# Attention with exponentials on two engines: a score ring of five PSUM banks and scores on demand for VectorE

## The chip, the cores and the metric

The kernel runs on one core of a Trainium2 chip. The time is that of one execution on the device, in microseconds (us). It is given as the median over several runs; beside it stands one execution that the hardware profiler recorded, with its own time. Most executions of one kernel agree within 0.3%.

## What is computed

The input is cut to what matters. S = 2048 rows, width D = 448, 16 heads of 28 columns, feed-forward width 1792, everything in bfloat16.

```python
xn = layernorm(x)
q, k, v = split(xn @ wqkv)                     # 16 heads of 28
p = softmax(q @ k.T * 28 ** -0.5)              # 2048 x 2048 a head
s = (p @ v).merge_heads() @ wo
g = silu(gelu(xn @ w1 + b1) @ w2 + b2)
out = x + s * g
```

## The kernel before

**Tiles.** A *score tile* is 128 keys by 512 queries of one head, as large as one PSUM bank. There are 16 blocks, one for each of 4 groups of 4 heads and 4 chunks of 512 queries; a block has 16 key tiles for each of its 4 heads, 64 score tiles. So there are 1024 of them, numbered m in the order of work, with block m // 64 and head m % 4. In the last block the tiles are cut by queries, so that its last quarters end one after another. For each tile TensorE computes the scores (line 1156), an engine takes the exponential, and TensorE multiplies it with the values and adds it into one accumulating bank, `acc` (PV, line 1389). At the end of a block VectorE copies `acc` out (line 1441) and the *epilogue* divides by the sums.

**Two engines take exponentials.** ScalarE does it in one ACTIVATE over several banks at once (line 1195), from the score ring to places in the buffer `P` (21 of them). VectorE does it for some tiles, called *late*, in four steps: it reads the bank and scales it into a buffer `y` (line 1218, 1309 for eight tiles), and then makes three passes over a pair of tiles (lines 1331, 1332, 1334), which leave the exponentials in one of five pair buffers `plate`. There are two `y` buffers, and one pair is in its three passes at a time.

**The ring.** PSUM has eight banks. Six are the ring, used as two sets of three: while ScalarE reads one set, TensorE fills the other. One is `acc`, and one, `misc`, is the *side bank*, for which all other work queues up: projections (line 722), values (976), feed-forward (1034, 1092), epilogues and the output projection (1480). The units of the ring are a fixed list, `UNITS`: two tiles each for the first 64 tiles (while banks 2 and 3 still serve the start), three behind them. When a unit is filled, `pick_late` may give its last tile to VectorE: then ScalarE's call covers two tiles, VectorE reads the third bank, and the set is free when both are done. At least three units lie between the two tiles of a pair. Eight late tiles are fixed beforehand (`MPAIRS`) and use the side bank, in block 9, where ScalarE does the gelus.

**The order of the work** is made when the kernel is built. Each part is a generator (`p_scores`, `p_exps`, `p_late`, `p_pv`, ...) that yields tasks with an engine, buffers, an estimated duration and a rank; a planner keeps a clock per engine, and puts next the task that can start first, by rank among those within 0.1 us of it. Each engine then runs its own list in that order, with semaphores between them. Late tiles are chosen by estimates: `backlog()` is VectorE's work that is due, `THS` has a limit on it for each block, and `SLACKS` says for each block how far VectorE may end behind ScalarE. Where TensorE would be idle for long by the planner, `p_busy` puts in keep-warm matmuls that add zero to `acc` (line 884).

**The gelu stretch.** In block 9, from tile GM = 582 on, ScalarE does all gelus together (line 1071): eight pieces from SBUF, and seven of three banks straight from the six banks of the ring (`p_direct`). Later `p_silu` uses tanh, which is in one table set with exp.

Of the kernel before, what the change touches and what calls it, by code (L numbers as in the profile page):

```python
# [24 lines left out]
UB = 3  # L25
# [6 lines left out]
MPAIRS = [tuple(64 * 9 + x for x in p) for p in ((16, 21), (26, 31), (36, 41), (46, 51))]  # L32
MLATE = set(m for ms in MPAIRS for m in ms)
_seq = [m for m in range(64, MTOT) if m not in MLATE]
UNITS = [list(range(m, m + 2)) for m in range(0, 64, 2)] + [_seq[i:i + UB] for i in range(0, len(_seq), UB)]
GU = min(u for u, ms in enumerate(UNITS) if ms[-1] >= GM)
RB, RPREV, UOF, UBASE, _last = {}, {}, {}, [], {}
for _u, _ms in enumerate(UNITS):
    UBASE.append(4 * (_u % 2) if _u < 32 else 3 * (_u % 2))
    for _k, _m in enumerate(_ms):  # L40
        UOF[_m] = _u
        RB[_m] = UBASE[_u] + _k
        RPREV[_m] = _last.get(RB[_m])
        _last[RB[_m]] = _m
for _m in sorted(MLATE):
    UOF[_m] = UOF[_m - 1]
LATE_GAP, LATE_SUB = 3, 15
LC = 1.85
THS = (5.0, 7.0, 15.0, 8.0, 8.0, 8.0, 8.0, 6.0, 8.0, 8.0, 8.0, 8.0, 8.0, 8.0, 8.0, 8.0)
SLACKS = (2.0, 2.0, 6.0, 2.0, -1.0, 2.0, 2.0, 2.0, 2.0, 1.0, 2.0, 2.0, 2.0, 4.5, 2.0, 2.0)  # L50
NU = len(UNITS)
# [24 lines left out]


class _Pair:
    __slots__ = ("i", "u", "ms", "done", "closed")

    def __init__(self, i, u, m):
        self.i, self.u, self.ms, self.done, self.closed = i, u, [m], 0, False
# [14 lines left out]
class _Kernel:  # L97
# [101 lines left out]

    def settle(self):  # L200
        again = True
        while again:
            again = False
            for p in sorted(self.procs, key=lambda p: (p[0], p[1])):
                op = p[3]
                if isinstance(op, _Task):
                    continue
                if op[0] == "until" and op[1]():
                    self.advance(p)
                    again = True  # L210
                elif op[0] == "bank" and self.banks and (len(op) < 2 or op[1]()):
                    i = min(range(len(self.banks)), key=lambda i: max(self.banks[i][1].tr, self.banks[i][1].tw or 0))
                    self.advance(p, self.banks.pop(i))
                    again = True
# [52 lines left out]
    def alloc(self):  # L267
# [60 lines left out]
        self.b_P = [B() for _ in range(NP)]  # L328
# [14 lines left out]
        self.b_xnT = [[B(), B()] for _ in range(C)]  # L343
        self.b_wqkf = B()
# [24 lines left out]
        self.b_dum = B()  # L369
        self.b_nm = [[B(), B()] for _ in range(C)]  # L370
# [13 lines left out]
    def schedule(self):  # L384
# [6 lines left out]
        K.sc_late = -1  # L391
        K.pv_u = -1
# [11 lines left out]
        K.ring6 = False  # L404
        K.taken = 0
        K.ring_rel = [False] * MTOT
        K.pv_done = [False] * MTOT
        K.late = set(MLATE)
        K.late_left = [len([m for m in MLATE if K.sub_of(m) == b]) for b in range(NBLK + 3)]
        K.late_q = deque()  # L410
        K.late_on = False
        K.open = None
        K.dve_q = 0.0
        K.PB, K.PPREV, K.plast, K.pptr = {}, {}, {}, 0
        K.act_ms, K.p0 = [None] * NU, [0] * NU
# [15 lines left out]
        K.spawn(K.p_take(3), 0)  # L431
# [4 lines left out]
        K.spawn(K.p_mlate(), 0)  # L436
# [433 lines left out]
    def pe_low(self):  # L870
        K = self
        now = max(K.tE[PE], K.now)
        while K.pe_hist and K.pe_hist[0][1] < now - HAM_WIN:
            K.pe_hist.popleft()
        return sum(b - max(a, now - HAM_WIN) for a, b in K.pe_hist) < (HAM_LOW if K.exp_u < NU - 20 else 1.1) * HAM_WIN

    def p_busy(self):
        K = self
        yield ("until", lambda: K.pv_u >= 0)
# [8 lines left out]
        while K.exp_u < NU - 2:  # L888
            yield ("until", lambda: K.pe_low() or K.exp_u >= NU - 2)
# [149 lines left out]
    def p_direct(self):  # L1039
        K = self  # L1040
        s0 = UBASE[GU - 1]
        for i, (c, f0) in enumerate(DIRECT):
            b0 = (s0 + 3 * i) % NRING
            yield ("until", lambda: K.exp_u >= GU - 1 + i if i < 2 else K.dir_read >= i - 1)
# [5 lines left out]
    def p_gelu(self):  # L1050
        K = self
        yield ("until", lambda: K.exp_u >= GU and K.n_f1 == len(SBT))
        left = [FT] * C
        s0 = UBASE[GU - 1]
        for q, pc in enumerate(PIECES):
# [4 lines left out]
            else:  # L1060
                i = K.dir_read
                yield ("until", lambda: K.dir_n > i)
# [78 lines left out]

    def p_scores(self):
        K = self
        for u in range(NU):
            ms = UNITS[u]
            fl, fm, rd = [], [], []
            ps = [(m,) + K.pieces(m) for m in ms]
            for k in range(4):
                for m, b, j, pc, _, _ in ps:
                    if k >= len(pc):  # L1150
                        continue
                    t, q0, nq, col = pc[k]
                    g, c = b // C, b % C

                    def f(eng, m=m, t=t, j=j, g=g, c=c, q0=q0, nq=nq, col=col):
                        return eng.matmul(K.ring[:, RB[m], col:col + nq],  # L1156
                                          K.kT[32 * j:32 * j + 32, g, t * 128:(t + 1) * 128],
                                          K.qT[32 * j:32 * j + 32, g, c * 512 + q0:c * 512 + q0 + nq],
                                          tile_position=(32 * j, 0), start=True, stop=True)
                    fl.append(f)  # L1160
                    fm.append(m)
                    rd += [K.b_qT[g][c], K.b_kT0 if (g, t // 2) == (0, 0) else K.b_kT[g][t // 4]]

            if len(ms) == 3 and not K.ring6:
                yield ("until", lambda: K.taken == 2)
                K.ring6 = True
            if u == GU + 1:
                yield ("until", lambda: K.dir_read == len(DIRECT))
            yield ("until", lambda: all(RPREV[m] is None or K.ring_rel[RPREV[m]] for m in ms))
            K.assign(u)  # L1170
            dur = 0.17 + 0.05 * len(ms) + 0.005 * (len(fl) - len(ms))
            for part in ([ms[-1:], ms[:-1]] if len(K.act_ms[u]) < len(ms) else [ms]):
                fp = [f for f, m in zip(fl, fm) if m in part]

                def fall(eng, fp=fp):
                    ins = None
                    for f in fp:
                        ins = f(eng)
                    return ins
                d = dur if part is ms else 0.12 if len(part) == 1 else dur - 0.12  # L1180
                yield _Task(PE, fall, rd, [K.b_ring[RB[m]] for m in part], d, 0.1, 1)
                if len(part) == 1:
                    K.sc_late = u
            K.sc_u = u

    def p_exps(self):
        K = self
        for u in range(NU):
            yield ("until", lambda: K.sc_u >= u)
            ms, b0, p0 = K.act_ms[u], UBASE[u], K.p0[u]  # L1190
            n = len(ms)
            yield ("until", lambda: all(K.PPREV[m] is None or K.pv_done[K.PPREV[m]] for m in ms))

            def fexp(eng, b0=b0, p0=p0, n=n):
                return eng.activation(K.P[:, p0:p0 + n, :], K.ring[:, b0:b0 + n, :], ACTF.Exp, scale=SM_SCALE)  # L1195
            yield _Task(ACT, fexp, [K.b_ring[b0 + k] for k in range(n)], [K.b_P[p0 + k] for k in range(n)],
                        0.0725 + 0.4267 * n, 0.08, 3)
            for m in ms:
                K.ring_rel[m] = True
            K.exp_u = u  # L1200
            K.exp_m = UNITS[u + 1][0] - 1 if u + 1 < NU else MTOT - 1
            if u >= NU - 2:
                for k in range(n):
                    K.banks.append((K.ring[:, b0 + k, :], K.b_ring[b0 + k]))

    def p_late(self):
# [6 lines left out]
        while K.sc_u < NU - 1 or K.late_q:  # L1213
            yield ("until", lambda: K.sc_u == NU - 1 or (K.late_q and UOF[K.late_q[0][0]] <= max(K.sc_u, K.sc_late)))
            if not K.late_q:
                return
            m, i, half, pair = K.late_q.popleft()
            yield _Task(DVE, lambda eng, m=m, i=i, half=half: eng.tensor_scalar(  # L1218
                K.ysb[i][:, 512 * half:512 * half + 512], K.ring[:, RB[m], :], SM_SCALE * LOG2E * 128.0,
                127.0 * 128.0, op0=ALU.mult, op1=ALU.add),  # L1220
                        [K.b_ring[RB[m]]], [K.b_y[i][half]], 0.69, 0.0, 1)
            K.dve_q -= 0.69
            K.ring_rel[m] = True
            pair.done += 1
            if pair.closed and pair.done == len(pair.ms):
                K.spawn(K.p_exp2(tuple(pair.ms), i), m)
# [11 lines left out]
    def close(self):  # L1238
        K = self
        p, K.open = K.open, None  # L1240
        p.closed = True
        if p.done == len(p.ms):
            K.spawn(K.p_exp2(tuple(p.ms), p.i), p.ms[-1])

    def pick_late(self, u):
        K = self
        ms = UNITS[u]
        m = ms[-1]
        sub = K.sub_of(m)
        if K.open and (u - K.open.u > LATE_GAP + 2 or K.sub_of(K.open.ms[0]) != sub):  # L1250
            K.close()
        n = 64 if sub < NBLK - 1 else 32
        r = m % 64
# [317 lines left out]
```

## Time and profile before

| | |
|---|---|
| median of 6 runs | 476.79 us (475.99 to 476.98) |
| the profiled execution | 476.78 us, its span 475.0 us |
| ScalarE | busy 462.4 us; first exponential at 13.0 us, last starts at 467.4 us |
| exponentials on ScalarE (L1195) | 350 calls, 420.6 us |
| VectorE | busy 378.9 us |
| late tiles: L1218 and L1309 | 86 and 8 |
| TensorE | busy 442.7 us, of which keep-warm (L884) 41.1 us |
| gelus (L1071) | first starts at 256.8 us, last at 281.4 us |

Names in the rows: PE is TensorE, PEld its weight loads, DVE VectorE, ACT ScalarE, POOL GpSimd, SP the queue of the transfers. A row of a group has line, engine, operation, output and input with shapes, the count, then busy time in us and the mean of one in ns, then the idle time of the engine ahead of it and who ended it. A row of waits has who waited for whom: total us, how often, the longest. A busy TensorE is modelled from starts, and overlapping calls of ScalarE count once in busy time but each in full in the mean. Buffers that share memory go by one name: late tiles' `y` is `x_sb`, the passes' `u` is `w` or `kT`.

### The profile page before, as it was taken

To read this page: it belongs to the slowest core of one execution; us is meant where nothing else is said; L and a number is where in the kernel's file an instruction comes from. 1 tells how busy PE (TensorE), PEld (TensorE's weight loads), DVE (VectorE), ACT (ScalarE), POOL (GpSimd) and SP (SyncE) were. 2 spreads that over 40 slices of the span, in tenths; PEclk is the share of its full clock that TensorE was granted. 3 is DMA by queue.
4 is the path that set the end of the run, shared out by engine and by line. 5 is a ranking of instruction groups with operands and counts; after the bars stand their busy time and mean duration, and the time that the engine had idled before them with its cause. 6 is when DMAs were issued, how large, how long until landed. Compare 5 with 4: busy or idle time off the path is not lost.

```text
span 475.0 us, 10008 instructions
## 1 busy us (share of the span) xinstructions
PE 442.7 (93%) x4185; PEld 165.7 (35%) x4185; DVE 378.9 (80%) x550; ACT 462.4 (97%) x394; POOL 39.8 (8%) x78
## 2 busy tenths in 40 slices
PE   6999999999999999999999989999999999999995
PEld 5443333333322233332223443233333233333453
DVE  8946979889886979897895939895795959899875
ACT  6999999999999999999999999999999999999994
POOL 7380001000100001000101000000100101010001
PEclk9999999999999999999999989999999999999999
DMA  8401000000000000001300000000010101011011
GB/s 266 137 7 31 2 0 1 1 1 3 1 1 0 1 1 1 1 2 25 113 1 0 1 1 1 1 1 1 1 40 1 40 1 40 1 59 39 23 41 40
DMA packets 8287, 11.08 MB, mean 23 GB/s; under 512 B 1649, under 2 KB 6897, under 8 KB 8242
## 3 DMA queue, kind: packets, MB, share of 16 engines
q1 hardware_dynamic: 7954, 9.75, 6.7%
q8 instruction: 33, 0.54, 0.5%
q10 hardware_dynamic: 288, 0.69, 0.4%
q14 instruction: 12, 0.10, 0.1%
HBM read 8.61 MB, written 1.84 MB: 22 GB/s over the span
## 4 chain that ended last, share of the span: by engine, by line
ACT 42%; PE 40%; issue 13%; DVE 4%; ACTq 0%; DVEq 0%
ACT P L1195 40%; PE ring L1156 11%; PE acc L1389 7%; PE misc L1092 5%; PE misc L1034 4%; PE acc L884 3%; PE misc L722 3%; PE ring L1034 1%; ACT h L1071 1%; PE misc L1480 1%; PE acc L866 1%; PE misc L976 1%; PE ring L722 1%; PE ring L976 1%; DVE kT L1331 0%
## 5 line engine op out<-in xcount | busy, mean ns | idle before, releaser
L1195 ACT ACTIVATE P<-ring 128x1536 bf16<-128x1536 f32 (+1 forms) x350 | 420.6, 1460 | 1.3 <-PE ring L1156 1.1
L1156 PE MATMUL ring<-qT,kT 32*128 32x512 bf16 (+2 forms) x1144 | 136.5, 360 | 20.7 <-ACT P L1195 15.5
L1389 PE MATMUL acc<-P,vaug 128*32 128x512 bf16 (+2 forms) x1055 | 95.9, 362 | 0.0
L1156 PEld LDWEIGHTS ring<-qT,kT 32*128 32x128 bf16 x1144 | 35.6, 91 | 129.7 <-ACT P L1195 119.0
L1218 DVE TENSOR_SCALAR x_sb<-ring 128x512 f32<-128x512 f32 x86 | 59.1, 687 | 26.6 <-PE ring L1156 25.7
L1092 PE MATMUL misc<-w,h 128*128 128x448 bf16 x224 | 51.7, 355 | 0.2 <-DVE w L1097 0.2
L1453 POOL CAST rhi<-rc 128x16 bf16<-128x16 f32 x15 | 10.4, 693 | 395.3 <-DVE rc L1451 296.1
L1389 PEld LDWEIGHTS acc<-P,vaug 128*32 128x32 bf16 x1055 | 24.8, 93 | 50.8 <-issue 45.1
L884 PE MATMUL acc<-ident,zero 128*128 128x128 bf16 x435 | 41.1, 224 | 0.0
L1034 PE MATMUL misc<-xnT,w 128*128 128x512 bf16 x140 | 38.7, 382 | 0.3 <-DVE h L1017 0.3
L884 PEld LDWEIGHTS acc<-ident,zero 128*128 128x128 bf16 x435 | 25.9, 99 | 20.8 <-issue 19.6
L1017 DVE CAST h<-misc 128x512 bf16<-128x512 f32 x35 | 24.0, 687 | 10.8 <-PE misc L1034 10.6
L1331 DVE SCALAR_TENSOR_TENSOR kT<-x_sb 128x1024 f32<-128x1024 uint16 (+1 forms) x28 | 31.9, 1140 | 0.7
L1332 DVE SCALAR_TENSOR_TENSOR kT<-kT 128x1024 f32<-128x1024 f32 (+1 forms) x28 | 31.8, 1137 | 0.4
L1331 DVE SCALAR_TENSOR_TENSOR w<-x_sb 128x1024 f32<-128x1024 uint16 (+1 forms) x22 | 25.7, 1167 | 0.4
L1332 DVE SCALAR_TENSOR_TENSOR w<-w 128x1024 f32<-128x1024 f32 (+1 forms) x22 | 25.7, 1170 | 0.2
L1092 PEld LDWEIGHTS misc<-w,h 128*128 128x128 bf16 x224 | 17.5, 97 | 23.7 <-issue 11.5
L1034 PE MATMUL ring<-xnT,w 128*128 128x512 bf16 x84 | 20.0, 380 | 0.6 <-ACT h L1071 0.6
L1334 DVE SCALAR_TENSOR_TENSOR x_sb<-kT,x_sb 128x1024 uint16<-128x1024 f32 (+1 forms) x16 | 19.0, 1187 | 0.2
L733 DVE TENSOR_SCALAR kT<-misc,ecol 128x512 bf16<-128x512 f32 x13 | 9.7, 747 | 9.0 <-PE misc L722 8.8
L1071 ACT ACTIVATE h<-h 128x2560 bf16<-128x2560 bf16 (+2 forms) x8 | 16.6, 2074 | 0.0
L722 PE MATMUL misc<-xnT,wq 128*128 128x512 bf16 x56 | 16.3, 400 | 0.2 <-DVE qT L962 0.2
(158 smaller groups left out, 433.7 us busy)
## 6 DMA issues: line engine op xcount, KB each, us to landing
h<-in_A_x_dram SPq DMA_DIRECT2D x4, 448.0 KB, 3.3
w<-in_B_w_dram SPq DMA_DIRECT2D x1, 1568.0 KB, 7.3
w<-in_B_w_dram SPq DMA_DIRECT2D x1, 1344.0 KB, 8.0
out_dram<-h SPq DMA_DIRECT2D x6, 224.0 KB, 1.9
x_sb<-in_A_x_dram SPq DMA_DIRECT2D x2, 448.0 KB, 5.3
h<-in_A_wqkv_dram SPq DMA_DIRECT2D x3, 168.0 KB, 5.1
x_sb<-in_A_x_dram ACTq DMA_DIRECT2D x1, 448.0 KB, 4.5
out_dram<-h SPq DMA_DIRECT2D x4, 112.0 KB, 1.7
```

The source lines that it names most:

```text
L722: ins = eng.matmul(bank, w[:, kt, g * 128:(g + 1) * 128], K.xnT[:, kt, c * 512:(c + 1) * 512], start=(kt == 0), stop=(kt == KT - 1))
L884: ins = eng.matmul(K.acc[:, 0:128], K.zero[:, :], K.ident[:, :], start=False, stop=True, skip_group_check=True)
L1017: yield _Task(DVE, lambda eng: eng.tensor_copy(dst, bank), [tok], wr, 0.69, 0.0, 2)
L1034: ins = eng.matmul(bank, K.w1[:, kt, ft * 128:(ft + 1) * 128], K.xnT[:, kt, c * 512:(c + 1) * 512], start=(kt == 0), stop=(kt == KT - 1))
L1071: yield _Task(ACT, lambda eng, dst=dst, src=src: eng.activation(dst, src, ACTF.Gelu_apprx_tanh), rd, K.b_hf[c][f0:f0 + n] + ([K.b_h[c]] if ...
L1092: ins = eng.matmul(ps, hv[:, ft, t * 128:(t + 1) * 128], K.w2[:, ft, :], start=(ft == 0), stop=(ft == FT - 1))
L1156: return eng.matmul(K.ring[:, RB[m], col:col + nq], K.kT[32 * j:32 * j + 32, g, t * 128:(t + 1) * 128], K.qT[32 * j:32 * j + 32, g, c * 51 ...
L1195: return eng.activation(K.P[:, p0:p0 + n, :], K.ring[:, b0:b0 + n, :], ACTF.Exp, scale=SM_SCALE)
L1218: yield _Task(DVE, lambda eng, m=m, i=i, half=half: eng.tensor_scalar(K.ysb[i][:, 512 * half:512 * half + 512], K.ring[:, RB[m], :], SM_SC ...
L1331: yield _Task(DVE, lambda eng: eng.scalar_tensor_tensor(u, lo, EXP_A, lo, op0=ALU.add, op1=ALU.mult), ty, [tu], d, 0.0, 4)
L1332: yield _Task(DVE, lambda eng: eng.scalar_tensor_tensor(u, u, EXP_B, u, op0=ALU.add, op1=ALU.mult), [tu], [tu], d, 0.0, 4)
L1389: return eng.matmul(K.acc[32 * j:32 * j + 32, q0:q0 + nq], K.vaug[:, t, 4 * g + j, :], ap[:, col:col + nq], tile_position=(0, 32 * j), sta ...
```

## The change

The list `UNITS` goes. Tiles are handed out by a counter, `next_m`. ScalarE's ring has five banks: sets 0 to 2 and 4 to 5, units of 3 and 2 in turn. Bank 3 joins the side bank, so that the general pool has two banks, except around the gelus, where `p_take3` takes it out. VectorE's process takes the next tiles off the counter itself when its backlog is low and a side bank is free, has TensorE score one or two of them into side banks, reads them, and starts the three passes of the pair at once. `MPAIRS` goes too; these tiles are chosen in the same way. `P`'s 21 places are joined by 21 in the feed-forward buffer `h` (from the start until shortly before the gelus) and 15 in `xnT` (behind the gelus); a unit takes the run of adjacent places that was used longest ago. PV may take late tiles early where all five pair buffers are full. The limits and slacks are new numbers: the slacks go from mostly 2 to mostly 6 to 8 us.

```diff
-THS = (5.0, 7.0, 15.0, 8.0, 8.0, 8.0, 8.0, 6.0, 8.0, 8.0, 8.0, 8.0, 8.0, 8.0, 8.0, 8.0)
-SLACKS = (2.0, 2.0, 6.0, 2.0, -1.0, 2.0, 2.0, 2.0, 2.0, 1.0, 2.0, 2.0, 2.0, 4.5, 2.0, 2.0)
+THS = (2.0, 5.0, 6.0, 6.0, 11.0, 8.0, 1.0, 5.0, 6.0, 6.0, 6.0, 5.0, 8.0, 6.0, 6.0, 6.0)
+SLACKS = (7.5, 6.0, 5.0, 7.0, 4.0, 7.0, 7.5, 7.0, 7.0, 8.0, 9.0, 10.0, 8.0, 7.0, 7.0, 2.5)
...
+        self.pslots = [(self.P[:, i0:i0 + n, :], k) for i0, n in ((0, NP),) for k in range(n)]
+        self.pslots += [(hx(2, 5, 9), k) for k in range(9)] + [(hx(3, 0, 12), k) for k in range(12)]
+        self.pslots += [(self.xnT[:, :, :].rearrange("p k (c n) -> p (k c) n", n=512), k) for k in range(16)]
...
     def p_gelu(self):
...
-                yield ("until", lambda: K.dir_n > i)
+                yield ("until", lambda: K.dir_n > i and K.room_free())
...
+    def p_take3(self):
+        K = self
+        K.bank3 = False
+        yield ("until", lambda: K.next_m >= GM - 12 and any(t is K.b_ring[3] for _, t in K.banks))
+        e = K.banks.pop([t is K.b_ring[3] for _, t in K.banks].index(True))
+        K.bank3 = True
+        yield ("until", lambda: K.dir_read == len(DIRECT))
+        K.banks.append(e)
...
     def p_scores(self):
...
+        u = 0
+        while K.next_m < MTOT:
+            yield ("until", lambda: K.exp_u >= u - 2)
...
+            b0 = 4 * (u % 2)
+            n = 2 if b0 or K.next_m < 64 else 3
+            if n == 3 and not K.taken:
+                yield ("until", lambda: K.taken == 1)
+            ms = list(range(K.next_m, min(K.next_m + n, MTOT)))
+            K.next_m += len(ms)
...
+            K.assign(ms, b0)
+            yield K.t_score(ms, {m: K.ring[:, b0 + k, :] for k, m in enumerate(ms)},
+                            [K.b_ring[b0 + k] for k in range(len(ms))], 0.17 + 0.05 * len(ms), 1)
...
     def p_late(self):
...
+        while not end():
+            yield ("until", lambda: end() or (len(K.ys) > 0 and len(K.banks) > 0 and K.pick(2)))
...
+            i = K.ys.pop(0)
...
+            while len(ms) < 2 and more():
...
+                got = [K.bank()]
+                if not ms and K.banks and K.sub_of(K.next_m + 1) == b:
+                    got.append(K.bank())
+                new = list(range(K.next_m, K.next_m + len(got)))
+                K.next_m += len(got)
...
+                yield K.t_score(new, {m: x[0] for m, x in zip(new, got)}, [x[1] for x in got], 0.22 + 0.03 * len(got), 0.9)
+                for m, (bank, tok) in zip(new, got):
...
+                    yield _Task(DVE, lambda eng, i=i, half=half, bank=bank: eng.tensor_scalar(
+                        K.ysb[i][:, 512 * half:512 * half + 512], bank, SM_SCALE * LOG2E * 128.0,
+                        127.0 * 128.0, op0=ALU.mult, op1=ALU.add), [tok], [K.b_y[i][half]], 0.69, 0.0, 1)
+                    K.dve_q -= 0.69
+                    K.banks.append((bank, tok))
+            K.spawn(K.p_exp2(tuple(ms), i), ms[-1])
+
+    def pick(self, k):
...
+        if not 0 < sub < NBLK or r < 4:
+            return False
+        left = (n - 1 - r) * 0.452 + SLACKS[m // 64]
+        if K.gu is not None and K.dir_read < len(DIRECT):
+            left += 2.0 * (len(DIRECT) - K.dir_read)
+        bl = K.backlog()
+        return (k == 1 or bl <= THS[m // 64]) and bl + k * (LC + 0.69) <= left
+
+    def p_room(self):
...
+        K.pon += [(NP, 9), (NP + 9, 12)]
+        yield ("until", lambda: K.next_m >= GM - 24)
+        K.pon = K.pon[:1]
+        yield ("until", lambda: K.gelu_done)
...
+        K.pon.append((NP + 21, 15))
...
     def p_pv(self):
...
-            yield ("until", lambda: K.exp_m >= ms[-1] and K.E_done >= first - 1)
+            go = lambda: K.exp_m >= ms[-1] and K.E_done >= first - 1
+            low = lambda: q % 16 > 0 and K.E_done >= first - 1 and not K.pls and len(mine()) > 3
+            while not go():
+                yield ("until", lambda: go() or low())
+                if not go():
+                    yield from self.pv_task(q, mine()[:4], [])
```

## The prediction

> **What bounds the kernel now.** I read the first table of the page, then the five stretches between the start and the tail (the table by windows), the groups of ScalarE by form, the waits of VectorE, and last the start and end of each single ACTIVATE and score matmul in the trace.
>
> The engines' totals:
>
> ```profile
> PE 442.7 (93%) x4185; PEld 165.7 (35%) x4185; DVE 378.9 (80%) x550; ACT 462.4 (97%) x394; POOL 39.8 (8%) x78
> ```
>
> ScalarE is busy 462.4 of 475.0 us. The stretches say whether that holds in each stage (columns: stretch, length, then busy us of PE, PE's weight loads, DVE, ACT, POOL):
>
> ```profile
> 42.00:250.00 208.00, 195.03 (x1792) 66.03 (x1791) 176.73 (x232) 207.87 (x172) 6.98 (x16) 1.00 0.03 9
> 250.00:290.00 40.00, 37.74 (x253) 15.27 (x250) 25.84 (x31) 38.84 (x27) 1.30 (x2) 0.96 0.00 1
> 290.00:330.00 40.00, 37.74 (x323) 12.74 (x320) 32.61 (x40) 40.00 (x34) 0.42 (x2) 1.00 0.01 1
> 330.00:400.00 70.00, 67.75 (x565) 23.13 (x566) 52.53 (x72) 70.00 (x58) 4.12 (x6) 1.00 0.07 21
> 400.00:450.00 50.00, 46.92 (x539) 17.93 (x537) 44.45 (x62) 50.00 (x42) 1.72 (x4) 1.00 0.09 29
> ```
>
> From 42 to 450 us ACT idles 1.3 us in all: it is the bound in every stage, and the time falls only by what is taken off ACT. DVE is busy 176.73 + 25.84 + 32.61 + 52.53 + 44.45 = 332.2 of these 408 us, 81%. That is the room to which tiles can go. The exponentials by form:
>
> ```profile
> L1195 ACT ACTIVATE P<-ring 128x1536 bf16<-128x1536 f32 x231 | 328.1, 1623 | 0.9 <-PE ring L1156 0.8
> L1195 ACT ACTIVATE P<-ring 128x1024 bf16<-128x1024 f32 x118 | 128.0, 1143 | 0.4 <-PE ring L1156 0.3
> ```
>
> 231 calls of three score tiles, 118 of two and one of one tile do 231*3 + 118*2 + 1 = 930 of 1024 tiles; VectorE does 94 (86 out of the ring, 8 out of the side bank). The means of 1.623 and 1.143 us are not prices, since consecutive calls overlap. Between the ends of neighbouring calls that were fed in time the trace has 1.343 us for three tiles and 0.917 us for two: 0.426 a tile and 0.065 a call. Check: 231*1.343 + 118*0.917 + 0.5 = 418.9, against 420.6 us of busy time of the line on the page. What VectorE's waits are for:
>
> ```profile
> DVE x_sb L1218 <- PE ring L1156: 25.7, 35, 3.1
> DVE h L1017 <- PE misc L1034: 10.6, 12, 1.7
> DVE kT L733 <- PE misc L722: 8.8, 4, 6.1
> DVE w L1097 <- PE misc L1092: 7.3, 6, 4.2
> ```
>
> The first is VectorE waiting for its own score tile, which today arrives only as the third bank of a ScalarE unit; the others wait for the one side bank, which is refilled only after VectorE has emptied it. These four alone are 52.4 us.
>
> **The change, part by part. (1) Units of 3 and 2.** After the first 64 tiles (units of 2 in both) a pair of calls does 5 tiles in 1.343 + 0.917 = 2.260 us, 0.452 a tile. Before, the 866 tiles behind the first 64 cost 418.9 - 32*0.917 = 389.6 us; with 3 and 2 they cost 866*0.452 = 391.4. So at an equal count of VectorE tiles the change loses **1.8 us**.
>
> **(2) Tiles on demand.** Each tile more on VectorE saves 0.452 us of ScalarE. It costs VectorE the reading of the scores (59.1 + 5.5 us) and three passes (57.7 at L1331, 57.7 at L1332, 57.8 at L1334): 237.8/94 = 2.53 us. Its other work between 42 and 450 is 332.2 - 237.8 = 94.4 us. At a busy share u of a window of 408 us less the gain g, VectorE takes L = (u*(408 - g) - 94.4)/2.53 tiles. What u will be the trace doesn't show; it bounds it. Lower end: 0.81, as now, if waits only change places. Its best 25 us now (400 to 425) have 22.58 us, 0.90, with 2.4 us still idle, and about half of that in waits for ring tiles; without those it is 0.95. A new pair is now asked for as soon as VectorE's backlog is under 5 or 6 us in most blocks, and a tile's score no longer waits for a ScalarE unit, so I take **0.93**, between the best window and that window without its ring waits; 0.97 is the upper end. With g = 4.5: L = (0.93*403.5 - 94.4)/2.53 = 111, 17 more than now: 17*0.452 = **-7.7 us**.
>
> **(3) The short window.** The set of 3 banks is now always refilled while a call of 2 tiles runs. In the trace a call may start until 0.10 us before the end of the one before it without delaying its end; so a refill has 0.917 - 0.10 = 0.81 us from the release of its banks. It needs 0.054 (semaphore to matmul), 0.39 (three matmuls side by side, starts 3 ns apart) and 0.045: 0.49. TensorE may come 0.32 us late; with the calls of 3, 0.75. What happens there now: of 70 calls of 3 behind a call of 2, 67 were not held up by over 20 ns. Counting all 314 refills from 45 us on, whatever their window, the last score matmul started later than a short window allows in 27; averaged over all refills that is 24 ns, and 5 ns without the six in which a tanh, the gelus or the table load stood between and nothing was late. With 111 tiles on VectorE there are (913 - 64)/5 = 170 short windows: 0.9 to 4.1 us. I take 8 ns, the mean of the stretch from 400 to 470 us: **+1.4 us**. It is no gain, since the refills of these stretches hold ACT up by next to nothing now.
>
> **(4) TensorE.** A refill holds TensorE 0.33 us (from its start to that of the next PV matmuls) whether 2 or 3 tiles wide. ACT's fills go from 350 to 32 + 340 = 372, and VectorE's now come apart in some 55 pairs: 77 more, 25 us. This replaces keep-warm matmuls (L884, 41.1 us) almost everywhere. Not from 330 to 400, where there are 0.7 us of them and TensorE has 2.3 us idle, against 12 or 13 more fills, 4.2 us. The second feed-forward product there ranks below scores and slips by 1 to 2 us to the stretch from 400 to 450, which has 6.1 us of them. I cost it at nothing; without that cover it is up to 4 us.
>
> **(5) More places for exponentials, the end of a block.** ACT's waits have no PV line at all, so places are no limit now and more of them give nothing by themselves. They are the cover for the larger slacks: VectorE may end a block 7 us behind, in which time ScalarE fills 7/0.452 = 15 more places, while PV stands at the block's last group, and so do the epilogue and the next block's PV behind it. 21 places less what PV is behind anyway may not hold that, 42 do. Cost: nothing; were the cover gone, ACT would wait for PV, by at most these 7 us in a block, and it would stand in its waits.
>
> **(6) The gelu stretch.** Eight side-bank tiles before; now as many as fit, still with one side bank, as bank 3 is lent to the gelus. The gelus' wait for places in h falls behind 24 tiles (10.8 us) in which no new ones are used. Nothing. The second weight load, on SP's queue at VectorE's first tile of block 8, has some 60 us until its first matmul. Start and tail are unchanged.
>
> Sum on the profiled execution, 476.78 us (475.0 of span and 1.8 around it; the median is 476.79): 476.8 - 7.7 + 1.8 + 1.4 = **472.3 us**.
>
> [...]
>
> **The rivals.** *VectorE fills up further* (u = 0.97): L = 116, 22 tiles, 476.8 - 9.9 + 1.8 + 1.4 = 470.1. For: 52 us of waits that two banks and a standing backlog address; against: no window today is above 0.90. Chance 0.17. *The demand isn't met*, so the change doesn't do what it says: VectorE's tiles compete with projections, feed-forward products and epilogues for the same two side banks, and u stays at 0.82 to 0.83. L = 96: 476.8 - 0.9 + 1.8 + 1.4 = 479.1. For: today a feed-forward tile holds its bank for 14 matmuls; against: the ring waits go in any case. Chance 0.09. Half of it (u = 0.86, L = 101) gives 476.8, chance 0.06. *ScalarE starves in the short windows*, the one that ends slower with VectorE full: each of 170 refills has 0.32 us of grace, and a feed-forward or projection task of TensorE lasts up to 0.5. Against the 7.7 - 1.8 = 5.9 us of gain it decides from 5.9/170 = 35 ns a window on; at 59 ns, what the refills from 330 to 400 average with the long ones counted, it costs 10 us: 481. For: TensorE gets 77 more fills; against: 67 of 70. Chance 0.10.
>
> **How the numbers follow.** My case (u from 0.88 to 0.95, 471 to 475.6) has 0.58. About 0.2%, 1 us, is what a measurement can tell here from no change. Faster takes my case and the fuller VectorE: 0.75; same 0.06; slower 0.19. The range reaches down to 469.0, past the fuller VectorE, and up to 478.8, nearly the unmet demand, leaving out the starved case and what lies beyond.
>
> **What would show it.** Right: the ACTIVATEs of the exponentials do about 913 tiles in some 372 calls, half of the later ones 1536 wide; VectorE's score reads rise from 94 to 106 to 114; its waits for them fall from 25.7 + 2.4 us to under 10; DVE's busy time rises by 30 to 45 us; ACT still has under 4 us of idle time between 42 and 450; L884 falls. Wrong: VectorE's score reads under 101 (step 2), or a wait of ACT for the ring's scores of 6 us and more (step 3), or one for PV (step 5).

## The result, and the profile after

The kernel after takes 479.27 us (median of 15 runs, 476.52 to 482.18); the kernel before takes 476.06 us (34 runs, 475.82 to 477.32). The ratio is 1.0063, interval 1.0047 to 1.0078: the change made the kernel slower by 0.6%. The profiled execution took 477.38 us, with a span of 475.6 us and a mean TensorE clock of 0.993.

The spread is itself a reading. Sorted by their mean clock, the 15 times lie in groups: 476.5 us at 0.997, 477.4 to 478.0 at 0.993 to 0.995, 479.2 to 479.3 at 0.990, 480.6 to 481.1 at 0.986 to 0.988, and 482.1 to 482.2 at 0.984. From group to group it is some 1.4 us. The profile shows what one step may be: a stretch of 3.41 us in which TensorE ran at half clock (from 421.40 us on, its clock 0.50; a *drop* below). One such drop lowers the mean clock of 475.6 us by 3.41/2/475.6 = 0.0036, about the distance of the groups; both profiles also end in such a stretch (clock 0.50 from 473.12 us on before, from 472.60 on after). The kernel before has two groups only, 475.8 to 476.3 and 476.7 to 477.3; its profiled execution, with one drop (at 282.0 us), is of the second.

The first table of the page shows that the work moved nearly as forecast, 29.5 us more on VectorE:

```profile
PE 447.0 (94%) x3990; PEld 157.6 (33%) x3990; DVE 408.4 (86%) x579; ACT 460.2 (97%) x417; POOL 46.8 (10%) x78
```

The five stretches of the table by windows, with the columns as before:

```profile
42.00:250.00 208.00, 199.90 (x1662) 61.71 (x1661) 189.33 (x256) 207.25 (x184) 10.47 (x16) 1.00 0.03 9
250.00:290.00 40.00, 37.60 (x249) 14.49 (x246) 29.05 (x33) 39.76 (x29) 1.28 (x2) 1.00 0.00 1
290.00:330.00 40.00, 39.40 (x301) 11.64 (x300) 36.12 (x44) 39.73 (x35) 1.07 (x2) 1.00 0.04 13
330.00:400.00 70.00, 67.32 (x568) 20.83 (x566) 61.60 (x78) 69.28 (x61) 4.25 (x6) 1.00 0.05 14
400.00:450.00 50.00, 44.28 (x481) 18.71 (x483) 44.14 (x57) 48.41 (x43) 4.55 (x4) 0.97 0.09 29
```

VectorE is busy 360.2 of the 408 us, 0.883 instead of 0.81. ScalarE is idle 3.6 us instead of 1.3, and 1.6 of these are in the last stretch, where the clock falls to 0.97 and TensorE is busy 44.28 us instead of 46.92. POOL, whose work there is unchanged (four instructions), takes 4.55 us instead of 1.72; before the gelus it takes 10.47 us instead of 6.98 for the same 16.

VectorE's score reads among its groups (line after 1236, was 1218 and 1309): 59 from the side bank `misc` and 49 from ring banks, of which bank 3 now is a side bank too.

```profile
L1236 DVE TENSOR_SCALAR x_sb<-misc 128x512 f32<-128x512 f32 x59 | 40.5, 686 | 6.1 <-PE misc L1144 4.1 <-PE ring L1144 1.6
...
L1236 DVE TENSOR_SCALAR x_sb<-ring 128x512 f32<-128x512 f32 x49 | 33.6, 687 | 11.5 <-PE ring L1144 10.5 <-PE misc L1144 0.4
```

That is 108 late tiles, and 916 in 373 calls on ScalarE. VectorE's longest waits:

```profile
DVE x_sb L1236 <- PE ring L1144: 12.1, 24, 1.7
DVE w L1078 <- PE misc L1073: 10.6, 4, 8.3
DVE E_sb L1434 <- PE acc L1374: 4.6, 8, 0.9
DVE x_sb L1236 <- PE misc L1144: 4.5, 11, 1.0
```

The waits for its own scores fell from 28.1 to 16.6 us, and a wait for the second feed-forward product has grown instead (10.6 us, one of 8.3). The waits of TensorE and of ScalarE hold what is new:

```profile
PE ring L1456 <- POOL rlo L1447: 2.8, 2, 1.6
PE misc L1456 <- POOL rlo L1447: 1.6, 1, 1.6
```

```profile
ACT xnT L1193 <- PE ring L1144: 1.9, 2, 1.4
ACT P L1193 <- PE ring L1144: 1.9, 4, 0.8
```

TensorE waits 4.4 us in three places for POOL, where the kernel before has 0.2 us. Line 1456 is the epilogue's matmul on the reciprocal of the sums, for which POOL makes a high part `rhi` and a rest `rlo`, two steps on 128x16. Both POOL groups, first of the kernel before and then of the kernel after:

```profile
L1453 POOL CAST rhi<-rc 128x16 bf16<-128x16 f32 x15 | 10.4, 693 | 395.3 <-DVE rc L1451 296.1 <-PE acc L884 55.8 <-PE acc L1389 43.3
...
L1454 POOL TENSOR_TENSOR rlo<-rc,rhi 128x16 bf16<-128x16 f32 x15 | 4.1, 276 | 1.2
```

```profile
L1446 POOL CAST rhi<-rc 128x16 bf16<-128x16 f32 x15 | 13.9, 927 | 392.5 <-DVE rc L1444 296.1 <-PE acc L1374 74.1 <-PE ring L1144 22.2
L1447 POOL TENSOR_TENSOR rlo<-rc,rhi 128x16 bf16<-128x16 f32 x15 | 7.7, 515 | 1.2
```

The means hide several prices: 0.20 to 0.22 us when VectorE is not in one of its passes over SBUF (the 13 `rlo` steps that lie wholly beside a score read of 0.69 us from PSUM take 0.22 us, as do the two with no VectorE instruction beside them), 0.26 us beside a pass of 0.36 us, 0.46 to 0.61 us beside a pass of some 0.6 us, and 1.06 to 1.20 us beside one of some 1.2 us. Of 30 steps, 9 took over 1 us before and 16 do after. So the high price stood in the trace of the kernel before. It cost nothing there because TensorE came to the epilogue 0.8 to 7.3 us behind the reciprocal, and POOL was done by then (but for the 0.2 us); after the change TensorE stands ready 0.6 to 0.9 us behind it in the last three epilogues, where POOL needs 1.7 to 2.4 us. The timeline of the worst of these places:

```profile
418.81 0.25 DVE L1444 RECIPROCAL rc<-ring 128x16 f32<-128x16 f32 x1
...
418.98 1.17 DVE L1312 SCALAR_TENSOR_TENSOR kT<-kT 128x1024 f32<-128x1024 f32 x1
419.13 1.08 POOL L1446 CAST rhi<-rc 128x16 bf16<-128x16 f32 x1 [22.25 <-PE ring L1144]
419.26 2.52 ACT L1193 ACTIVATE xnT<-ring 128x1536 bf16<-128x1536 f32 x2
...
420.19 1.23 DVE L1314 SCALAR_TENSOR_TENSOR plx<-kT,x_sb 128x1024 uint16<-128x1024 f32 x1
420.29 1.20 POOL L1447 TENSOR_TENSOR rlo<-rc,rhi 128x16 bf16<-128x16 f32 x1
...
421.55 0.30 PE L1456 MATMUL misc<-ident,rhi 128*32 128x128 bf16 x4 [1.57 <-POOL rlo L1447]
...
422.52 0.61 PE L1144 MATMUL ring<-qT,kT 32*128 32x512 bf16 x4
...
423.21 1.45 ACT L1193 ACTIVATE xnT<-ring 128x1536 bf16<-128x1536 f32 x1 [1.43 <-PE ring L1144]
```

Each of these two POOL steps ends 0.06 to 0.07 us behind the VectorE pass that it overlaps (419.13 + 1.08 = 420.21 and 418.98 + 1.17 = 420.15; then 421.49 and 421.42); over all slow steps of both profiles it is 0.05 to 0.08. So `rlo` is there 2.4 us behind the reciprocal. TensorE, which works in the planned order, stands at the matmuls on it for 1.57 us; the score matmuls queued behind come late, and ScalarE waits 1.43 us. Why POOL ends with the pass, no run here shows.

The clock drops there as well, from 421.40 on. The stretch of 3.42 us ahead of the drop, with PE first of the busy times:

```profile
417.98:421.40 3.42, 2.00 (x20) 0.63 (x19) 3.39 (x4) 3.42 (x4) 2.19 (x2) 1.00 0.02 5
```

TensorE was busy 2.00 of 3.42 us. The drop behind it lasts 3.41 us. By the profiles of this case the drops came behind stretches that were 0.36 (before_slower_pool, 1.22 of 3.40 us) to 0.68 busy (tuned2_sd, 2.33 of 3.41 us).

To compare kernels I use ScalarE's *held-up time*: the distance between the ends of neighbouring calls less 1.343 us (three tiles) or 0.917 us (two), summed. It is 2.23 us before and 7.97 us after, of which 2.7 us come in the three epilogues with TensorE waiting for POOL (0.24, 1.54, 0.94).

### The profile page after: what moved, and what is told of

Read it like the earlier page. It is cut to its first block, busy times and chain, and to the rows that moved or that the text cites. A ratio compares the mean times of both kernels' runs of the same rounds, so it can differ in the third digit from the quotient of the medians.

```text
span 475.6 us, 9572 instructions
## 1 busy us (share of the span) xinstructions
PE 447.0 (94%) x3990; PEld 157.6 (33%) x3990; DVE 408.4 (86%) x579; ACT 460.2 (97%) x417; POOL 46.8 (10%) x78
## 4 chain that ended last, share of the span: by engine, by line
PE 50%; ACT 34%; issue 11%; DVE 3%; POOL 1%; ACTq 0%; DVEq 0%
ACT P L1193 16%; PE ring L1144 15%; PE acc L1374 10%; ACT h L1193 9%; ACT xnT L1193 5%; ACT h L1052 3%; PE ring L1073 3%; PE misc L1073 3%; PE ring L1014 2%; PE acc L864 2%; PE ring L702 2%; PE misc L1014 2%; PE misc L702 2%; PE ring L956 1%; PE misc L956 1%
## 5 line engine op out<-in xcount | busy, mean ns | idle before, releaser
L1193 ACT ACTIVATE P<-ring 128x1024 bf16<-128x1024 f32 (+1 forms) x206 | 245.7, 1304 | 2.4 <-PE ring L1144 1.9
L1193 ACT ACTIVATE h<-ring 128x1024 bf16<-128x1024 f32 (+1 forms) x101 | 115.3, 1234 | 0.2
L1193 ACT ACTIVATE xnT<-ring 128x1536 bf16<-128x1536 f32 x66 | 77.2, 1314 | 2.1 <-PE ring L1144 1.9
L1374 PE MATMUL acc<-P,vaug 128*32 128x512 bf16 (+2 forms) x587 | 68.3, 362 | 0.6 <-DVE E_sb L1434 0.6
L1236 DVE TENSOR_SCALAR x_sb<-misc 128x512 f32<-128x512 f32 x59 | 40.5, 686 | 6.1 <-PE misc L1144 4.1
L1236 DVE TENSOR_SCALAR x_sb<-ring 128x512 f32<-128x512 f32 x49 | 33.6, 687 | 11.5 <-PE ring L1144 10.5
L1311 DVE SCALAR_TENSOR_TENSOR kT<-x_sb 128x1024 f32<-128x1024 uint16 x31 | 37.8, 1220 | 0.9
L1312 DVE SCALAR_TENSOR_TENSOR kT<-kT 128x1024 f32<-128x1024 f32 x31 | 37.5, 1211 | 0.3
L1374 PE MATMUL acc<-h,vaug 128*32 128x512 bf16 x235 | 36.1, 388 | 0.0
L1073 PE MATMUL ring<-w,h 128*128 128x448 bf16 x112 | 29.3, 356 | 0.0
L864 PE MATMUL acc<-ident,zero 128*128 128x128 bf16 x240 | 20.7, 222 | 0.0
```

Source lines behind the costliest of these rows:

```text
L864: ins = eng.matmul(K.acc[:, 0:128], K.zero[:, :], K.ident[:, :], start=False, stop=True, skip_group_check=True)
L1073: ins = eng.matmul(ps, hv[:, ft, t * 128:(t + 1) * 128], K.w2[:, ft, :], start=(ft == 0), stop=(ft == FT - 1))
L1193: return eng.activation(reg[:, i0:i0 + n, :], K.ring[:, b0:b0 + n, :], ACTF.Exp, scale=SM_SCALE)
L1236: yield _Task(DVE, lambda eng, i=i, half=half, bank=bank: eng.tensor_scalar(K.ysb[i][:, 512 * half:512 * half + 512], bank, SM_SCALE * LOG ...
L1311: yield _Task(DVE, lambda eng: eng.scalar_tensor_tensor(u, lo, EXP_A, lo, op0=ALU.add, op1=ALU.mult), ty, [tu], d, 0.0, 4)
L1312: yield _Task(DVE, lambda eng: eng.scalar_tensor_tensor(u, u, EXP_B, u, op0=ALU.add, op1=ALU.mult), [tu], [tu], d, 0.0, 4)
```

## The experiments

Theory A: the epilogue's two POOL steps, slow beside a fuller VectorE, hold TensorE in its order; that delays ScalarE and leaves TensorE too little to do in the stretch ahead of a drop (2.00 of 3.42 us above; the next expectation calls it a clock window). Theory B: too few keep-warm matmuls (20.7 us instead of 41.1) let the clock drop, and POOL's waits are incidental. Beside both stands theory C, the prediction's own step 3: refills that come late in the short windows.

**POOL's steps on VectorE (steps_dve).** All else keeps its planned order; the two POOL tasks remain in the plan as empty entries.

```diff
-        yield _Task(DVE, lambda eng: eng.reciprocal(K.rc[:, :], bank[:, 0:16]), ...)
+        def frec(eng, n=2 * b):
+            eng.reciprocal(K.rc[:, :], bank[:, 0:16]).then_inc(K.s_rc, 1)
+            eng.wait_ge(K.s_rc, n + 1)
+            eng.tensor_copy(K.rhi[:, :], K.rc[:, :]).then_inc(K.s_rc, 1)
+            eng.wait_ge(K.s_rc, n + 2)
+            return eng.tensor_tensor(K.rlo[:, :], K.rc[:, :], K.rhi[:, :], ALU.subtract)
+        yield _Task(DVE, frec, ...)
```

> The changed kernel with the epilogue's two steps on POOL (the cast to rhi, the subtraction to rlo) done on VectorE right behind the reciprocal; the planned order of everything else is the same to the last task. Theory A (VectorE's long passes slow these two POOL steps from 0.2 to 1.1 or 1.2 us each; TensorE, in order, then waits up to 1.65 us at the ends of three blocks, which holds up the scores and empties a clock window): TensorE's 4.4 us of waiting for POOL goes, ScalarE's held-up calls lose some 3 us, the clock's mean stays at 0.994 or above in nearly every execution instead of 0.984 to 0.997; 473 to 474.5 us. Theory B (too few keep-warm matmuls, as there are 240 instead of 435, whatever POOL does): clock still scattered from 0.984 to 0.997, 477 to 481. Theory C (the refills in the short windows are the loss): clock is beside the point, 476 and more.

475.11 us (474.86 to 475.34), ratio 0.997 (0.9959 to 0.9982), clock 0.999 to 1.0 in every run. The same stretch in its table by windows:

```profile
417.98:421.40 3.42, 3.35 (x59) 1.32 (x56) 3.32 (x6) 3.42 (x5) 0.00 (x0) 1.00 0.02 5
```

TensorE is busy 3.35 instead of 2.00 us, the drop is gone, and held-up time falls to 5.07 us. Keep-warm is unchanged (240 matmuls, 20.5 us), so B falls. What is left is mostly C's: of the 5.07 us, 4.3 lie in the 170 calls of three behind a call of two. The time is above what A expected by about the price of the edit itself, which the next run gives.

**The same edit in the kernel before (before_steps_dve).**

> Control: the same edit in the kernel before, planned order unchanged. TensorE waits for POOL only 0.2 us there. Theory A: within 0.1% of the kernel before. If the edit itself gains or costs (15 times some 0.3 us of VectorE), it shows here, by at most 1 us.

477.55 us, ratio 1.0024 (1.0015 to 1.0033): the edit costs some 1.3 us where there is no POOL wait to remove, more than the 1 us that was expected at most. Two steps of 0.17 us and their waits, 15 times, are added to VectorE.

**More keep-warm (ham95).** The planner's threshold for them goes up; the plan puts 131 tasks of them instead of 107.

```diff
-HAM_WIN, HAM_LOW, DUM = 3.4, 0.85, 0.17
+HAM_WIN, HAM_LOW, DUM = 3.4, 0.95, 0.17
```

> The changed kernel with the planner's threshold for keep-warm matmuls at 0.95 instead of 0.85 of its window: 131 keep-warm tasks instead of 107, 108 tiles on VectorE as in the changed kernel, 1.0 us more planned. Theory A: a wait of TensorE for POOL can't be filled by matmuls that stand behind it in order, so the waits and the scatter of the clock stay: 476.5 to 481. Theory B: clock at 0.997 in all executions, 476 to 477. Theory C: as the changed kernel without drops of the clock, 476.5 to 478.

480.28 us, ratio 1.0069 (1.0046 to 1.0092), clock 0.988 to 0.995: no better. The waits stand among TensorE's as before:

```profile
PE ring L1456 <- POOL rlo L1447: 2.5, 2, 1.3
```

A keep-warm matmul is queued behind the waiting one like everything else, so it can't fill that gap: the three waits are 2.5 + 1.3 = 3.8 us, 4.4 in the kernel after. The profile shows a second thing: this execution, the fastest of the four at 478.09 us, has no drop before the last 5 us, yet the second and third of its waits for POOL (1.3 us each) hold ScalarE up by 0.96 and 1.24 us. So a wait for POOL cost time without a drop too; in the profile of the kernel after, one of the three was followed by a drop (at 421.40 us).

**Without the added places (pl21).** The lines `K.pon += [(NP, 9), (NP + 9, 12)]` and `K.pon.append((NP + 21, 15))` go.

> The changed kernel with the 21 places for exponentials of before alone. By the prediction's step 5 the added places give nothing by themselves but cover VectorE's larger slacks at the ends of blocks: without them ScalarE waits for PV at the ends of blocks, up to 7 us in each. The planner with 21 places has ScalarE idle 17 us instead of 3, in gaps of 2 to 3.6 us at the ends of blocks, and ends 12 us later (with 113 tiles on VectorE). Theory A and C alike: 486 to 492 us. If the places are not needed: under 480.

494.73 us, ratio 1.0378 (1.0332 to 1.0424). ScalarE's waits:

```profile
ACT P L1193 <- PE acc L1372: 12.7, 4, 3.9
ACT P L1193 <- PE ring L1144: 8.5, 9, 1.8
```

Line 1372 is PV (the matmul with the values): the wait that the prediction named as the sign of a lost cover, 12.7 us in four. The places are needed at these slacks. The run came out slower than expected, with a clock of 0.971 to 0.990 and 5.9 us of waits for POOL.

**Demand capped at 94 tiles, steps on VectorE (cap94_sd).** This takes the gain away and leaves the price of the rest.

```diff
-        if not 0 < sub < NBLK or r < 4:
+        if not 0 < sub < NBLK or r < 4 or len(K.late) > 94 * (m - 64) / 928:
```

> The changed kernel with the POOL steps on VectorE, and with VectorE's demand capped along the way so that it takes 93 tiles, about the 94 of before: what the five-bank ring costs by itself. Theory A with the prediction's steps 1 and 3 (a refill of 3 in a call of 2 comes late, steps_dve has 2.8 us more held-up time than before): 476.1 + 1.8 (units) + 0.4 (a tile) + 1.2 (the edit's own price in the control) + 2 to 3 = 481.5 to 483; the plan itself is 481.0. Rival D (VectorE's fuller load is what costs, by contention, and the ring is free): no slower than 478. ScalarE's held-up time over 2 us more than before under A, under 1 us more under D.

480.86 us (480.65 to 481.67) with 93 tiles, ratio 1.0102. That is a little under the range of A and far above D's 478; the held-up time, 1.4 us more than before, lies between what the two expected. Above the kernel before it is 4.65 us; the units make 1.8, one tile less 0.45, the edit 1.3, the held-up time 3.66 - 2.23 = 1.4: 4.95 in sum. From here to steps_dve, 15 more tiles bring 5.75 us, 0.38 each instead of 0.452.

**Shorter tasks on TensorE (split_sd and split).** Feed-forward and value tasks become single matmuls of 0.18 to 0.25 us, so that a refill comes in between; split_sd has the steps on VectorE, split leaves them on POOL. Limits and slacks are those of the change.

```diff
-        for k in range(2):
-            yield K.t_f1(c, ft, bank, tok, k)
+        for k in range(KT):
+            yield K.t_f1(c, ft, bank, tok, k, 5, True)
...
-        for q in range(7):
+        for q in range(FT):
```

> As steps_dve, but TensorE's feed-forward and value tasks are put into the order as single matmuls (0.18 to 0.25 us) instead of in twos and fours (0.4 to 0.8), so that less can stand ahead of a refill; 109 tiles on VectorE, planned 0.5 us later than steps_dve. If the remaining 2.8 us of held-up calls come from such tasks in front of refills of 3 in a call of 2: held-up time falls from 5.1 to 2.5 to 3.5 us, 473 to 474.5 us. If TensorE's load as such is behind it: unchanged, 475 to 476.

473.70 us, ratio 0.9953 (0.9939 to 0.9967), held-up time 3.40 us as expected, 109 tiles.

> split_sd with the two epilogue steps back on POOL, the same planned order: what POOL costs in another order than that of the changed kernel. Theory A: one or more waits of TensorE for POOL of over 1 us, clock scattered or low, 475 to 479 us against 473.7. If the steps on VectorE brought their gain by something that holds for the changed kernel's order alone: no slower than 473.7, perhaps 1 us faster, as VectorE is spared 15 times some 0.45 us.

473.31 us (473.02 to 474.42), ratio **0.9936** (0.9921 to 0.995): this version beats both kernels. A's case of the expectation was wrong, and the other one came true. POOL is still slow (850 and 415 ns), but in this order TensorE comes to the epilogue 1.1 to 7.3 us behind the reciprocal and always after POOL, and no wait for POOL is left. So A needs a condition: a slow POOL costs only where the order puts TensorE's matmuls within POOL's 2.4 us. Beside split_sd, moving the steps to VectorE costs 0.4 us in this order, not 1.3.

**A slower POOL in the kernel before.** The rival direction of A: with the old units and choice of tiles, make POOL late by small extra copies ahead of the cast, 3 (before_slow_pool), then 12 (before_slower_pool).

```diff
+            for i in range(12):
+                eng.tensor_copy(K.junk[:, b, i, :], K.rc[:, 0:1])
```

> The kernel before, order unchanged, with three further small POOL copies (4 columns each, 0.2 us alone, about 1.1 beside a pass of VectorE) ahead of the cast in each of 15 epilogues. Theory A, that a late POOL makes TensorE wait in order and this both holds up ScalarE and drops TensorE's clock, must then show in the kernel before too, which has no short windows and 94 tiles on VectorE: from the reciprocal's end to the epilogue's TensorE matmuls there are 2 to 4 us there in 12 of 15 cases, and POOL would now need 1.2 to 5; so some 5 to 9 waits of 0.5 to 3 us, 480 to 490 us, clock 0.975 to 0.99. If only the changed ring is sensitive (Theory C): within 1 us of before, clock as before.

476.62 us beside 476.53, ratio 1.0000: no effect. POOL was done 0.9 to 4.2 us behind the reciprocal, still ahead of TensorE in nearly all epilogues, so this tested nothing.

> With three extra copies POOL was done 0.9 to 4.2 us behind the reciprocal and still ahead of TensorE in 14 of 15 epilogues of the kernel before, so nothing was tested. Now twelve copies of one column (0.18 us each): POOL done 2.6 us behind the reciprocal, 3.5 us and more beside one of VectorE's passes. TensorE comes at 1.9 to 2.8 us in eight epilogues, at 0.9 in the last and at 3.0 to 3.6 in four. Theory A: waits of TensorE of 0.3 to 2 us in 8 to 12 epilogues, 8 to 14 us in all; ScalarE held up after each wait of over 0.7 us; 479 to 486 us and a mean clock under 0.994. If a wait of TensorE for POOL is hidden (ScalarE has a unit ready, and the clock doesn't mind): under 477.5 and a clock of 0.994 to 1.0 as before.

488.72 us, ratio 1.0242 (1.0194 to 1.029), clock 0.975 to 0.988. TensorE's and ScalarE's waits, and the stretches ahead of two of its clock drops:

```profile
PE misc L1468 <- POOL rlo L1459: 12.2, 9, 2.2
```

```profile
ACT P L1196 <- PE ring L1157: 10.6, 17, 1.9
```

```profile
50.69:54.10 3.41, 1.36 (x41) 0.71 (x41) 2.05 (x3) 2.33 (x3) 1.91 (x2) 1.00 0.00 0
453.50:456.90 3.40, 1.22 (x47) 0.69 (x44) 1.92 (x2) 2.32 (x3) 2.56 (x13) 1.00 0.00 0
```

The whole chain of A appears in a kernel that has no part of the change, larger than expected: 12.2 us of TensorE's waits, 14.3 us held up, drops behind stretches 0.40 and 0.36 busy. The copies did not act by slowing VectorE: its passes take 1.216 us in the mean, as in the kernel before.

**Three plans chosen anew.** The limits `THS` and `SLACKS` were chosen again for the split versions: tuned_sd with the planner's price of a call at the measured 0.0655 + 0.426 a tile, tuned2_sd with the old price, tuned_pool with the steps on POOL and counted at 1.1 and 1.2 us instead of 0.2 and 0.22.

> split_sd with the planner's price of an exponential set to the measured one (0.0655 + 0.426 a tile instead of 0.0725 + 0.4267) and limits and slacks chosen anew for the planned end, 468.7 instead of 472.1 us; 109 tiles. If the order was off because ScalarE runs ahead of the planner's clock: the chip keeps to within 1 us of the plan and takes 470.5 to 473 us. If not: 474 to 476 as before it.

474.42 us (474.06 to 476.53), ratio 0.9972. The last instruction of an engine ends at 469.9 us of the profile, 1.2 us behind the planned end; the span is 2.5 us longer than that, and 1.8 us lie around it, which the expectation doesn't seem to count. The held-up time is 4.44 us, and no gain over split_sd is left.

> The two epilogue steps stay on POOL, but the planner counts them at 1.1 and 1.2 us instead of 0.2 and 0.22, so that TensorE's matmuls behind them are put later; single matmuls as in split_sd, limits and slacks chosen anew for this plan (469.7 us planned, 111 tiles). Theory A: no wait of TensorE for POOL over 0.3 us, clock 0.994 and above, 472 to 474.5 us. If POOL on VectorE's side matters in another way than by TensorE's wait: drops of the clock as in the changed kernel and 476 or more.

473.79 us (472.53 to 473.86), ratio 0.9942. No wait for POOL is above 0.3 us, as A says of a plan that knows the price. The clock is 0.989 in three of four, though, with a drop at 281.1 us, at the end of the gelus: that part was missed.

> split_sd (steps on VectorE, single matmuls) with limits and slacks chosen anew for this plan, with the planner's old price of an exponential, which leaves ScalarE running ahead of the plan and so some grace to the refills: planned end 470.6 instead of 472.1 us, 109 tiles as in split_sd. If chip and plan keep their distance of split_sd: 472.2 us. If the choice only shifts stalls, as in tuned_sd: 473.5 to 475.

476.05 us (472.73 to 476.51), ratio 0.9976, slower than either case of the expectation: four runs at 472.7 to 473.7 and eight at 475.7 to 476.5 with a lower clock. Its profile has a drop at 205.7 us behind a stretch 0.68 busy. Why this plan drops so often stays open.

## Why the prediction was wrong

**The step that failed is the cover of the epilogue.** Step 5 moved the block's end and the epilogue behind later tiles and costed that at nothing as long as ScalarE had places; pl21 shows the cover of places was real. But the epilogue is a chain over VectorE, POOL and TensorE, and the prediction priced neither a POOL step beside a VectorE that runs more of its SBUF passes nor the place where TensorE waits for it. The held-up time of that is 7.97 - 5.07 = 2.9 us, one clock drop in the profile included. It belongs to this planned order and not to five banks or demand as such: split has the units, the places, the limits and the slacks of the change, and no wait for POOL. How the planner came to put TensorE there stays open. The drops of the other executions, which the median holds and the profile doesn't, were in no step. None of the three signs of being wrong that the prediction names appears: there are 108 score reads, ScalarE waits 3.8 us for the ring's scores, and not at all for PV.

**Step 1** (units, +1.8 us) held: the spacing of calls is still 1.343 and 0.917 us, and cap94_sd adds up with it.

**Step 2** was mis-sized: 108 tiles instead of 111, and 14*0.452 = 6.3 us instead of 7.7, with u = 0.883 instead of 0.93. By the step's formula 0.883 gives only 104 tiles. But VectorE's busy time between 42 and 450 us grew by 360.2 - 332.2 = 28.0 us for 14 tiles, 2.0 each instead of 2.53: the price of a tile was too high, and this made up for about four of the seven tiles that the lower u took. That the step missed by three tiles only is in part luck; why a tile came cheaper isn't shown. The score waits fell to 16.6 us, not under 10, and the wait for the second feed-forward product grew from 7.3 to 10.6.

**Step 3** was mis-sized within its bounds: 5.07 - 2.23 = 2.8 us instead of 1.4, and 25 ns a short window (4.3 us in 170) instead of 8. The 8 ns were a mean over refills of every kind of window; the 70 short ones of the kernel before had 17 (1.2 us). With 93 tiles (cap94_sd) the addition is 1.4 us. Shorter tasks on TensorE (split_sd) take it to 3.40 - 2.23 = 1.2, which fits refills that waited for tasks of up to 0.5 us, as the starved rival had it, at a fraction of its size.

**Step 4** held: keep-warm fell from 41.1 to 20.7 us at no cost that a run shows, as steps_dve runs at full clock (0.999 to 1.0) with as few.

**The sum** by what was measured is -6.3 + 1.8 + 2.8 + 2.9 = +1.2 us; the spans of the two profiles differ by 0.6. The medians differ by 3.2, since the profile after lies 1.9 under its median and the one before 0.7 above its own. That the 1.9 are one or two more drops is read from the clock of those runs, not from a trace. Against the forecast, steps 2 and 3 are each 1.4 us short, the waits for POOL add 2.9, and the median adds 1.9. Without the waits for POOL, steps_dve less the price of its edit (1.3 us in the kernel before, 0.4 in the split order) would be an estimated 473.8 to 474.7; the terms as measured give 476.06 - 6.3 + 1.8 + 2.8 = 474.4. That is the prediction's mechanism with its two sizes corrected, and a gain of some 2 us instead of 4.5.

The measured time is that of the rival *demand isn't met* (479.1), but not for its reason, so the agreement is luck: the demand was met to more than four fifths (14 of 17 tiles).

## What to carry to other kernels

Before filling an idle engine, look for small steps of another engine that an in-order engine waits for, and read their time by what runs beside them: the mean of 276 ns stood for fourteen steps of 0.22 us and one of 1.07. In a planned order, count such a step at its slow price or keep its user away from it; split did the second, and tuned_pool the first. And where executions of one kernel spread in steps, set the mean clock beside each: here the steps were worth more than the effect that was forecast.

## What the runs showed of the hardware

POOL's 128x16 steps took 0.20 to 0.22 us in the two profiles, or ended 0.05 to 0.08 us behind the VectorE pass over SBUF (0.36, 0.6 or 1.2 us) that they overlapped; the 13 that lay wholly beside a score read from PSUM (0.69 us) took 0.22 us. The drops of the clock to 0.50 lasted 3.41 us, in one case 6.83 (tuned_pool at 281.1 us, mean clock 0.989), behind stretches in which TensorE was 0.36 to 0.68 busy. The share alone didn't decide: a stretch of 0.60 was followed by a drop in the kernel before (278.56 to 281.97 us), and one of 0.60 (394.10 to 397.50) and one of 0.51 (448.30 to 451.70) by none in the kernel after. In the kernel after, a drop goes with some 1.4 us of time, an estimate from the groups of its executions.
